# Pooled attention followed by a token and channel mixer on one core: contiguous stationary operand for the maxima, four groups of U turned by VectorE from a DRAM scratch, the order of all steps read from a table

## The chip, the core and the metric

One core of a Trainium2 chip runs the kernel alone. The metric is device time in microseconds, the median of three runs. Engines: PE (matrix products; PEld is its weight load), DVE (vector), ACT (scalar), POOL (GpSimd) and SP, which here only issues DMAs. Each engine has one list of instructions, in the order in which the program wrote them, so that an instruction that waits holds up those behind it in its list; for SP that is a DMA behind a DMA.

## The reference, cut to what matters

```python
def _attn_ref(q, k, v):                      # 4 batches, 8 heads, 1152 positions, 64 channels
    q_pool = q.reshape(B, H, S // 2, 2, D).mean(axis=3)
    scores = scale * np.matmul(q_pool, k.transpose(0, 1, 3, 2))
    scores = scores - np.max(scores, axis=-1, keepdims=True)
    attn = np.exp(scores)
    attn = attn / (np.sum(attn, axis=-1, keepdims=True) + 1e-09)
    return np.matmul(attn, v)
...
def _moe_ref(x, w_tok1, w_tok2, w_ch1, w_ch2):   # x: 4 x 576 x 512
    xt = x.transpose(0, 2, 1)
    h = np.maximum(xt @ w_tok1, 0.0) @ w_tok2
    u = x + h.transpose(0, 2, 1)
    h2 = np.maximum(u @ w_ch1, 0.0) @ w_ch2
    return u + h2
```

The mixer's weights come as 64-bit floats and are narrowed on the chip.

## The kernel before

Everything is split into a high half (rounded for PE) and a low half (the rest), and products are summed from two or three matmuls. There are 32 heads, taken one after the other, two heads to a pair p.

For a pair, K and the pooled Q are loaded in blocks of 32 channels (tiles kn, qn), added (qp, line 594), turned by DVE in 32x32 blocks (line 619 for K) and split (kh, kl; qh, ql). DMAs then stack the halves of one head under each other (kk, qq, and k2, q2 for the third term).

The maxima of a head (maximum, line 758) come first: for each block c of 128 query rows and each third n of the keys, one matmul of 384 columns, with the queries as the stationary operand, and one DVE reduction of its output (line 760). Blocks 0 to 3 take the queries as `QQ[i3][:, c:4 * P:4]`, so with a step of four elements; the rest of 64 rows of both heads of a pair stands in a contiguous tile qd. A DVE reduction makes mh of it (line 725), and one DMA moves its four columns into row 64 of q2 (line 732), where the maximum is subtracted as one more channel of the scores; a second DMA moves the rest (line 736). With the step of four, partition p of mh holds the rows 4p to 4p+3, and the DMA moves runs of four elements.

The scores (line 824) go to PSUM, ACT takes the exponential twice (pf, ph), the low half pl = pf - ph is made by POOL or by DVE (line 845), and PE multiplies with V (line 870). A head named in IN_PV takes three matmuls for this, one of which also sums the row's denominators; any other head takes two, and DVE sums the denominators instead (line 852, six reductions a head), combines two halves (line 883) and, after five more transposes on PE, adds up (lines 919, 922). The output is normalised into U. After every fourth head follows a half of a batch's token mix (lines 952 to 995).

At the end come 24 blocks of channel weights, narrowed by ACT, DVE and POOL, and the channel mix: U is turned in six groups of 384 rows (make_ut, on PE, lines 1060 to 1071, four blocks of 128 channels each), then two chains of matmuls (lines 1082 and 1110) for groups 0 and 1 while weights arrive, and for groups 2 to 5 one after the other.

The program's order is made by a planner: each step has an engine, a cost, a due time from the table DUE and the steps that it depends on; run() picks, step by step, the one that can start first by its own clock, and steps that fit POOL or DVE go where they end first. Three banks of PSUM (ring r) serve the maxima, the turned blocks and the mixer.

Of the kernel before, what the change touches and what calls it, by code (L numbers as in the profile page):

```python
# [3 lines left out]

# [6 lines left out]
F32 = mybir.dt.float32  # L11
# [22 lines left out]
    "scores": -4.5,  # L34
    "p_lo": 5.87,
    "sum": -9.78,
    "pv": 0.35,
    "o": -76.73,
    "finish": -37.65,
    "max": -26.5,  # L40
    "max_each": 0.65,
    "prep": -47.86,
    "v": 2.17,
    "stack": 17.09,
    "stack_2": 76.73,
    "mix": 4.49,
    "mix_x": 5.65,
    "w_tok": 7.87,
    "w_tok_each": 1.94,
    "w_bits": -174.47,  # L50
    "sum_each": 1.52,
    "pv_lo": 0.35,
    "lo_first": 5.54,
    "max_first": -15.11,
    "max_second": 6.31,
    "scores_each": -3.1,
    "p_hi": 0.54,
    "pv_one": -0.55,
    "finish_each": -3.1,
    "den_sum": -15.08,  # L60
    "x_lo": -44.24,
    "x": 27.99,
    "den": -30.38,
    "rd": -20.25,
    "u": 23.45,
    "u_each": -41.15,
    "max_of": -11.3,
    "max_row": -21.2,
    "max_first_each": 11.02,
    "q_pool": -54.73,  # L70
    "q_turn": 5.19,
    "k_each": 1.94,
    "k_hi": 4.75,
    "k_turn": -0.25,
    "q_diag": -18.19,
    "k_lo": -10.58,
    "q_hi": -15.28,
    "q_lo": -11.2,
    "load_kq": -56.71,
    "load_v": -34.48,  # L80
    "v_lo": -62.7,
    "load_w_tok": -85.57,
    "mix_x_lo": -44.87,
    "mix_1": 3.42,
    "mix_t": -1.29,
    "mix_2": 3.13,
    "mix_u": -203.98,
    "w_ch": 9.35,
    "w_ch_each": 23.09,
    "ut_0": -20.54,  # L90
    "ut_1": -43.87,
# [4 lines left out]
IN_PV = (0, 1, 2, 3, 5, 8, 10, 12, 13, 14, 16, 18, 21, 22, 23, 24, 26, 27, 31)  # L96
# [9 lines left out]
class Step:  # L106


    __slots__ = ("eng", "cost", "other", "shared", "fn", "at", "n", "get", "bufs", "next", "left", "ready", "end")


class Plan:
# [11 lines left out]
    def step(self, eng, cost, fn, at, read=(), write=(), get=(), after=(), other=None, shared=False):  # L124
# [6 lines left out]
        s.other, s.shared = other, shared or eng == POOL  # L131
# [36 lines left out]
    def run(self):  # L168
        clock, wire, port = [0.0] * 6, 0.0, 0.0

        def wake(s):
            ready[s.eng].append(s)
            if s.other:
                ready[s.other[0]].append(s)

        slots = {k: [(0.0, i) for i in range(len(v))] for k, v in self.pools.items()}
        ready = [[] for _ in range(6)]
        turns = {k: deque() for k in self.pools if k not in self.any_order}
        for s in self.steps:
            for buf in s.get:  # L180
                if buf.pool in turns:
                    turns[buf.pool].append(buf)
            if not s.left:
                wake(s)
        order = []
        while len(order) < len(self.steps):
            best = None
            for eng in range(6):
                for s in ready[eng]:
                    start = max(s.ready, clock[eng])  # L190
                    if s.shared:
                        start = max(start, port)
                    if s.other:
                        ends = [
                            max(s.ready, clock[e]) + cost
                            for e, cost in ((s.eng, s.cost), s.other)]
                        if (ends[0] > ends[1] + self.stay) == (eng == s.eng):
                            continue
                    for buf in s.get:
                        free = slots[buf.pool]  # L200
                        if not free or buf.pool in turns and turns[buf.pool][0] is not buf:
                            start = float("inf")
                        else:
                            start = max(start, min(free)[0] + 200)
                    key = (start, s.at, s.n)
                    if best is None or key < best[0]:
                        best = key, s, eng
            (start, _, _), s, eng = best
            assert start < float("inf")
            ready[s.eng].remove(s)  # L210
            if s.other:
                ready[s.other[0]].remove(s)
                if eng != s.eng:
                    s.eng, s.cost = s.other
            for buf in s.get:
                free = slots[buf.pool]
                buf.slot = min(free)[1]
                free.remove(min(free))
                if buf.pool in turns:
                    turns[buf.pool].popleft()  # L220
            if s.eng == DMA:
                clock[DMA] = start + 650
                wire = max(start + 1265, wire) + s.cost
                s.end = wire + 650
            else:
                s.end = clock[s.eng] = start + s.cost
                if s.shared:
                    port = s.end
            for t in s.next:
                t.ready = max(t.ready, s.end + AFTER.get((s.eng, t.eng), 0))  # L230
                t.left -= 1
                if not t.left:
                    wake(t)
            for buf in s.bufs:
                buf.left -= 1
                if not buf.left:
                    slots[buf.pool].append((max(u.end for u in buf.users), buf.slot))
            order.append(s)
        self.span = max(s.end for s in order)
        return order  # L240
# [3 lines left out]
def kernel(  # L244
# [43 lines left out]
    due = DUE  # L288
    WARM = 11
    KEEP = (0, 1, 2, 3)  # L290
# [85 lines left out]
    identr = const.tile([P, P], F32R, name="identr")  # L376
    ve.tensor_copy(identr, ident)
# [73 lines left out]
    for i in range(2):  # L451
# [30 lines left out]
    def tok_weights(after):  # L482
# [6 lines left out]
        def load(key, dst, src, n, write):  # L489
            raw[key] = dst  # L490
            step(DMA, wire(n), lambda: sy.dma_start(dst, src), due["w_tok"] + due["load_w_tok"], write=write,
                 after=after)
# [60 lines left out]
    def load_kq(p, t, after):  # L553
        b, h0 = divmod(2 * p, H)

        def load_k(j, c0, c1):
            step(DMA, 2 * wire(4 * P * (c1 - c0) * D), lambda: sy.dma_start(
                KN[:, c0:c1, j], k[b, h0 + j].rearrange("(c p) d -> p c d", p=P)[:, c0:c1]),
                t, write=[("kn", j, c, y) for c in range(c0 // 3, c1 // 3) for y in range(2)], after=after)

        def load_k_blocks(j, y):
            g = slice(64 * j + 32 * y, 64 * j + 32 * y + 32)
            step(DMA, 2.1 * wire(4 * S * 32), lambda: sy.dma_start(
                KB[g], k[b, h0 + j].rearrange("(m r) (y i) -> y r m i", r=32, y=2)[y]),
                t, write=[("kn", j, c, y) for c in range(3)], after=after)

        def load_q_blocks(j, y, x):
            g = slice(64 * j + 32 * y, 64 * j + 32 * y + 32)
            step(DMA, 2.1 * wire(4 * SQ * 32), lambda: sy.dma_start(
                QB[g, x], q[b, h0 + j].rearrange("(m r x) (y i) -> x y r m i", r=32, x=2, y=2)[x, y]),  # L570
                t, write=[("qn", j, y, x)], after=after)
# [649 lines left out]
```

## Time and profile before

| what | value |
|---|---|
| median of 3 runs | 932.87 us (928.86 to 935.71) |
| the profiled execution | 930.23 us |
| its span, first to last instruction | 928.4 us |
| PE busy | 888.6 us, 96% |
| DVE, ACT, POOL busy | 621.6, 552.3, 502.7 us |
| granted PE clock, mean | 0.984 |

Busy time is the time in which at least one instruction of an engine was under way. Matmuls overlap, so that a single matmul's duration is longer than its distance to the next; what a matmul costs in a dense stretch is read from the distances of the starts.

### The profile page before, as it was taken

How to read it: one execution, taken by the hardware profiler on the slowest of the kernel's cores; microseconds unless marked ns; L12 is line 12 of the kernel's file. 1: busy time of each engine (PE TensorE's matmuls, PEld its weight loads, DVE VectorE, ACT ScalarE, POOL GpSimd, SP SyncE). 2: the span in 40 equal slices, each digit the busy share in tenths (PEclk: the TensorE clock that was granted, in tenths of full speed). 3: DMA queues.
4: the chain of work that ended last, by engine and by line, in shares of the span. 5: the costliest groups of instructions: out<-in, count | busy, mean ns of one | idle time of the engine just before them, and what ended most of it. 6: DMA issues, size and time to landing. Idle time of an engine off the chain costs nothing.

```text
span 928.4 us, 15308 instructions
## 1 busy us (share of the span) xinstructions
PE 888.6 (96%) x5399; PEld 827.3 (89%) x5399; DVE 621.6 (67%) x1193; ACT 552.3 (59%) x1141; POOL 502.7 (54%) x394
## 2 busy tenths in 40 slices
PE   8579999999999999999999999999999999999997
PEld 6479989898989999989999999889899999999996
DVE  7777888987978889898788878678992222221211
ACT  5667888788698779787878789754332111111110
POOL 4778798877688778787688778733330000000000
PEclk9879999999999999999999999999999999999999
DMA  8988757745577557575665352034430101000001
GB/s 169 194 161 151 147 119 153 135 99 107 120 149 137 117 114 140 120 149 99 140 124 104 82 119 83 18 114 125 131 114 1 69 1 35 1 35 1 35 1 34
DMA packets 218348, 91.56 MB, mean 99 GB/s; under 512 B 194016, under 2 KB 201568, under 8 KB 218272
## 3 DMA queue, kind: packets, MB, share of 16 engines
q1 hardware_dynamic: 218272, 90.60, 46.6%
q8 instruction: 42, 0.69, 0.3%
q14 instruction: 34, 0.28, 0.1%
HBM read 43.25 MB, written 4.72 MB: 52 GB/s over the span
## 4 chain that ended last, share of the span: by engine, by line
PE 72%; DMA 9%; DVE 7%; ACT 6%; SPq 3%; issue 2%; POOL 1%; DVEq 0%; ACTq 0%; POOLq 0%
PE o L870 15%; PE r L1082 14%; PE s L824 12%; PE s L1110 11%; PE r L758 10%; DMA kk<-kl 5%; PE o L1110 2%; PE r L985 2%; DMA raw<-in_moe_w_ch_dram 2%; ACT pf L838 2%; ACT ph L841 2%; PE r L967 2%; DVE mx L760 1%; PE r L907 1%; DVE v L364 1%
## 5 line engine op out<-in xcount | busy, mean ns | idle before, releaser
L845 POOL TENSOR_TENSOR pl<-pf,ph 128x576 fp32r<-128x576 f32 x258 | 372.5, 1463 | 99.1 <-PE o L870 56.8
L838 ACT ACTIVATE pf<-s 128x576 f32<-128x576 f32 x288 | 195.4, 682 | 75.7 <-PE s L824 66.3
L760 DVE TENSOR_REDUCE mx<-r 128x1 f32<-128x384 f32 x384 | 199.4, 550 | 43.0 <-PE r L758 39.4
L841 ACT ACTIVATE ph<-s 128x576 fp32r<-128x576 f32 x288 | 189.3, 660 | 11.1 <-PE o L870 7.4
L870 PE MATMUL o<-ph,vv 128*65 128x288 f32 (+2 forms) x918 | 192.4, 299 | 3.4 <-DVE ot L883 1.7
L824 PE MATMUL s<-qq,kk 128*128 128x288 f32 x574 | 170.0, 306 | 3.1 <-ACT ph L841 1.3
L758 PE MATMUL r<-kk,qq 128*128 128x384 f32 x372 | 159.3, 448 | 9.7 <-DMA kk<-kl 8.2
L824 PE MATMUL s<-q,k 65*128 65x288 f32 x576 | 167.9, 301 | 0.3 <-ACT q L793 0.3
L1090 DVE SCALAR_TENSOR_TENSOR h<-r,h 128x384 fp32r<-128x384 f32 x72 | 40.1, 556 | 166.3 <-ACT h L1088 166.2
L1088 ACT ACTIVATE h<-r 128x384 fp32r<-128x384 f32 x72 | 35.3, 491 | 186.2 <-PE r L1082 186.2
L870 PEld LDWEIGHTS o<-ph,vv 128*65 128x65 f32 (+2 forms) x918 | 132.4, 152 | 9.8 <-DVE ot L883 3.6
L870 PE MATMUL o<-pl,vv 128*65 128x288 f32 (+1 forms) x576 | 134.9, 296 | 0.1
L1110 PE MATMUL s<-w,h 128*128 128x512 f32 x504 | 130.8, 394 | 0.0
L758 PEld LDWEIGHTS r<-kk,qq 128*128 128x128 f32 x372 | 112.6, 312 | 17.8 <-issue 6.0
L824 PEld LDWEIGHTS s<-qq,kk 128*128 128x128 f32 x574 | 112.9, 197 | 10.2 <-ACT ph L841 6.0
L824 PEld LDWEIGHTS s<-q,k 65*128 65x128 f32 x576 | 111.0, 193 | 0.7 <-ACT q L793 0.5
L1082 PE MATMUL r<-big,w 128*128 128x384 f32 x576 | 109.1, 337 | 0.3 <-DVE h L1090 0.3
L1110 PEld LDWEIGHTS s<-w,h 128*128 128x128 f32 x504 | 93.4, 188 | 16.5
L1082 PEld LDWEIGHTS r<-big,w 128*128 128x128 f32 x576 | 101.7, 188 | 4.1 <-DVE h L1090 0.5
L852 DVE TENSOR_REDUCE sum<-pf 128x96 f32<-128x960 f32 x78 | 88.1, 1135 | 4.6 <-ACT pf L838 4.5
L870 PEld LDWEIGHTS o<-pl,vv 128*65 128x65 f32 (+1 forms) x576 | 87.6, 161 | 1.6 <-DVE pl L845 0.3
L1045 POOL TENSOR_TENSOR w<-v,w 128x512 fp32r<-128x512 f32 x24 | 33.9, 1416 | 60.2 <-ACT w L1044 60.2
(131 smaller groups left out, 1119.5 us busy)
## 6 DMA issues: line engine op xcount, KB each, us to landing
raw<-in_moe_w_ch_dram SPq DMA_DIRECT2D x24, 512.0 KB, 3.6
kk<-kh SPq DMA_DIRECT2D x32, 288.0 KB, 4.0
qq<-qh SPq DMA_DIRECT2D x64, 144.0 KB, 2.5
kk<-kl SPq DMA_DIRECT2D x32, 288.0 KB, 4.5
vn<-in_v_dram SPq DMA_DIRECT2D x32, 288.0 KB, 3.2
k<-kk SPq DMA_DIRECT2D x31, 288.0 KB, 5.1
kn<-in_k_dram SPq DMA_DIRECT2D x60, 144.0 KB, 4.2
qn<-in_q_dram SPq DMA_DIRECT2D x120, 72.0 KB, 2.7
```

What stands on the lines that cost most here:

```text
L758: step(PE, mm(SP3), lambda ps=ps, w=w, x=x: te.matmul(at(ps)[:, 0:SP3], w, x, start=True, stop=True), t, read, [ps], [ps])
L760: step(DVE, dve(SP3), lambda ps=ps, m=m: ve.tensor_reduce(m, at(ps)[:, 0:SP3], axis=AX.X, op=ALU.max), t + due["max_of"], [ps], [key])
L824: te.matmul(at(st)[:, i, 0:HF], w[:, c * P:(c + 1) * P], x[:, fq * HF:(fq + 1) * HF], start=(n == 0), stop=(n == len(terms) - 1))
L838: step(ACT, act_ps(2 * HF) + (0 if near else 49), lambda pf=pf, st=st: sc.activation(pf, at(st)[:, :, 0:HF], AF.Exp, scale=ESC), t, [(st, ...
L841: step(ACT, act_ps(2 * HF) + 15, lambda ph=ph, st=st: sc.activation(at(ph), at(st)[:, :, 0:HF], AF.Exp, scale=ESC), t + due["p_hi"], [(st, ...
L845: both(2 * HF, lambda e, pf=pf, ph=ph, pl=pl: e.tensor_sub(at(pl), pf, f(at(ph))), t + due["p_lo"], [("pf", s), ph], [pl], [pl], on=POOL i ...
L852: step(DVE, 65 + 1.06 * (NK + 1) * HF // CUT, lambda fq=fq, cs=cs: ve.tensor_reduce(SUM[:, fq, cs], PF[:, 5 * fq:5 * fq + 5, cs].rearrange ...
L870: lambda o=o, x=x, w=w, m=m, i=i, c=c, new=new, end=end: te.matmul(at(o)[0:m - w], VV[i2][:, c, w:m], at(x)[:, i], start=new, stop=end),
L1082: te.matmul(at(ps)[:, 0:GT], w[:, c], x[:, c], start=(c == 0 and n == 0), stop=(c == NC4 - 1 and n == 2))
L1088: step(ACT, act_ps(GT), lambda: sc.activation(at(h)[:, 0], at(ps)[:, 0:GT], AF.Relu), t, [ps], [h])
L1090: step(DVE, dve(GT), lambda: ve.scalar_tensor_tensor(out=at(h)[:, 1], in0=at(ps)[:, 0:GT], scalar=0.0, in1=f(at(h))[:, 0], op0=ALU.max, op ...
L1110: te.matmul(at(ps), a[:, x * P:(x + 1) * P], w, start=(fi == 0 and m == 0), stop=(fi == NF - 1 and m == 2))
```

## The change

1. The maxima's queries become contiguous: block c is now rows 128c to 128c+127, and partition p of mh holds rows p, 128+p, and so on. Each of the four columns of mh is moved by a DMA of its own, 128 single elements each.
2. The token mix also stores U to a DRAM scratch (MIXED), with two DMAs for each of its eight halves. For groups 2 to 5 of the channel mix, make_ut loads each block of 128 channels back with four DMAs of 32 channels each (runs of 128 bytes) and turns it with one DVE instruction; PE's transposes stay for groups 0 and 1. The first product of a group waits for all four blocks of its U.
3. run() no longer plans. A table gives the order of all 6869 steps, and a second one names the 62 that go to DVE and not to POOL. Buffers are given out in the order in which they come free.
4. IN_PV has 17 heads and not 19. DUE's numbers changed, but with the table they no longer set the order. An unused copy of the identity goes, and three of the first head's extra warming matmuls.

Read out, the second table puts on DVE 41 low halves of P, 2 of V, 9 of the token mix, 5 sums of Q and 5 of the channel weights (in the kernel before: 30, 5, 5, 5 and 0). Between the loads of pair 1 and the first DMA of the row of maxima of head 1, the first table puts on SP two of the four loads of token weights, two of the four kn of pair 2 and its eight qn. In the kernel before, all four loads of token weights stand there, all four kn and eight qn of pair 2, and two qd of pair 1. On PE the first step after head 0 is now a score of head 1; before, it was a maximum of head 2 with qd.

```diff
-IN_PV = (0, 1, 2, 3, 5, 8, 10, 12, 13, 14, 16, 18, 21, 22, 23, 24, 26, 27, 31)
+IN_PV = (0, 1, 2, 4, 8, 10, 13, 16, 18, 20, 21, 22, 24, 26, 28, 30, 31)
...
     def run(self):
...
+        near = np.frombuffer(zlib.decompress(base64.b85decode(ORDER)), np.uint8).reshape(2, -1)
+        order = [self.steps[n] for n in np.cumsum(near.T.copy().view("<i2")[:, 0])]
+        assert len(set(order)) == len(self.steps)
+        for n in OTHER:
+            self.steps[n].eng, self.steps[n].cost = self.steps[n].other
+        slots = {k: deque(range(len(v))) for k, v in self.pools.items()}
+        for s in order:
+            assert not s.left
             for buf in s.get:
...
+                buf.slot = slots[buf.pool].popleft()
             for t in s.next:
...
                 t.left -= 1
...
             for buf in s.bufs:
                 buf.left -= 1
                 if not buf.left:
...
+                    slots[buf.pool].append(buf.slot)
         return order
...
-    KEEP = (0, 1, 2, 3)
+    KEEP = (0, 1, 2)
...
+    dram = ctx.enter_context(tc.tile_pool(name="dram", bufs=1, space=bass.MemoryType.DRAM))
+    MIXED = dram.tile([B * SQ, C], F32, name="mixed")
...
+        "l": [f(x).rearrange("p j c -> p (j c)")[:, 0:GT] for x in (T1H, T1L)],
...
-        step(DMA, 300, lambda: sy.dma_start(
-            row[:, 0:4 * P].rearrange("o (p c) -> o p c", c=4), mh[:, 0:4]), t,
-            [("mh", 0)], [("row", h % 2, c) for c in range(4)])
+        for c in range(4):
+            step(DMA, 300, lambda c=c: sy.dma_start(row[:, c * P:(c + 1) * P], mh[:, c:c + 1]), t,
+                 [("mh", 0)], [("row", h % 2, c)], pieces=P)
...
-                w, x = QQ[i3][:, c:4 * P:4], KK[i3][:, ks]
+                w, x = QQ[i3][:, c * P:(c + 1) * P], KK[i3][:, ks]
...
+        m0 = g * 2 * SQ
+        step(DMA, 1.3 * wire(16 * P * CM), lambda: sy.dma_start(
+            MIXED[m0 + c0 * P:m0 + (c0 + 4) * P, cols].rearrange("(c p) x -> p c x", p=P),
+            u[:, c0:c0 + 4, cols]), t + due["mix_u"], [("out", b, i, c) for c in range(4)], [("mixed", b, i, 0)],
+             pieces=4 * P)
...
+            if first:
+                def turn(ps=ps, c=c):
...
+                step(PE, G * TURN, turn, t, read + ["first"], [ps, key, *old.get(i, ())], [ps])
+            else:
+                lb, row = Buf("l"), (18 * g + 2 * n * G) * REM
+                for a in range(4):
+                    col = c * P + 32 * a
+                    step(DMA, 2.45 * wire(4 * 32 * GT), lambda lb=lb, a=a, row=row, col=col: sy.dma_start(
+                        at(lb)[32 * a:32 * a + 32].rearrange("r (m i) -> r m i", i=32),
+                        MIXED[row:row + GT, col:col + 32].rearrange("(m r) i -> r m i", r=32)),
+                        t + due["ut_load"], read, [(lb, a)], [lb] if a == 0 else [], after=mixes, pieces=GT)
+                step(DVE, 1.2 * GT, lambda ps=ps, lb=lb: ve.transpose(at(ps)[:, 0:GT], at(lb)), t,
+                     [*((lb, a) for a in range(4)), "first"], [ps, key, *old.get(i, ())], [ps])
...
-            step(PE, 3 * mm(GT), part, t, [("ut", i % 3, c), ("w", 3, fi), "rest"], [ps, h],
+            step(PE, 3 * mm(GT), part, t, [*(("ut", i % 3, x) for x in range(NC4)), ("w", 3, fi), "rest"], [ps, h],
```

## Rows read from the trace of the kernel before

**Rows 1.** The page, part 1: busy time, share of the span, instructions.
```profile
...
PE 888.6 (96%) x5399; PEld 827.3 (89%) x5399; DVE 621.6 (67%) x1193; ACT 552.3 (59%) x1141; POOL 502.7 (54%) x394
...
```

**Rows 2.** Windows by stage: length, busy us (instructions) per engine, granted clock, DMA.
```profile
...
20.00:50.00 30.00, 18.62 (x105) 16.11 (x105) 21.90 (x54) 18.85 (x45) 23.49 (x21) 0.82 1.04 187
50.00:80.00 30.00, 26.73 (x135) 24.33 (x134) 23.41 (x53) 19.07 (x39) 22.30 (x18) 0.79 0.79 155
60.00:600.00 540.00, 523.60 (x3542) 501.27 (x3542) 448.40 (x871) 441.34 (x913) 428.88 (x325) 1.00 0.61 119
...
700.00:860.00 160.00, 160.00 (x818) 145.25 (x817) 33.10 (x60) 22.14 (x46) 0.00 (x0) 1.00 0.06 20
...
```

**Rows 3.** Line 758 (maxima): instructions, duration ns minimum/median/maximum.
```profile
...
L758 PEld LDWEIGHTS r<-kk,qq x372: 307/309/337, 19.7 to 572.3; 128*128 128x128 f32 x186
...
L758 PEld LDWEIGHTS r<-kh,qd x48: 186/188/330, 15.7 to 532.7; 128*128 128x128 f32 x48
...
```

**Rows 4.** PE in order of time around 405 us: start, us, line, operands, count.
```profile
...
405.55 0.43 PE L758 MATMUL r<-kk,qq 128*128 128x384 f32 x1
405.82 0.29 PE L870 MATMUL o<-pl,vv 128*128 128x288 f32 x1
...
```

**Rows 5.** The same around 435 us.
```profile
...
434.75 0.34 PE L758 MATMUL r<-kh,qd 128*128 128x384 f32 x1
434.93 0.30 PE L824 MATMUL s<-qq,kk 128*128 128x288 f32 x1
...
```

**Rows 6.** The chain of waits, 740 to 765 us: start, us, what.
```profile
...
748.04 2.10 PE r L1082 x12
...
756.41 0.98 PE r L1060 x9
...
```

**Rows 7.** The chain of waits, whole span.
```profile
...
134.89 1.06 PE o L870 x8
...
```

**Rows 8.** Groups by line, DVE: count, busy us, mean ns, idle before.
```profile
...
L760 DVE TENSOR_REDUCE mx<-r 128x1 f32<-128x384 f32 x384 | 199.4, 550 | 43.0 <-PE r L758 39.4
...
L852 DVE TENSOR_REDUCE sum<-pf 128x96 f32<-128x960 f32 x78 | 88.1, 1135 | 4.6 <-ACT pf L838 4.5
...
L883 DVE TENSOR_TENSOR ot<-o,low 64x288 f32<-64x288 f32 x26 | 11.6, 445 | 4.0 <-ACT low L881 3.7
...
L919 DVE TENSOR_REDUCE r<-r 128x4 f32<-128x512 f32 x13 | 9.0, 691 | 4.2 <-PE r L915 3.2 <-PE r L907 0.9
...
```

**Rows 9.** Line 845 (low half of P): instructions on POOL and DVE, ns.
```profile
...
L845 POOL TENSOR_TENSOR pl<-pf,ph x258: 1399/1447/2626, 18.8 to 598.9; 128x576 fp32r<-128x576 f32 x129
...
L845 DVE TENSOR_TENSOR pl<-pf,ph x30: 740/784/1981, 144.3 to 597.4; 128x576 fp32r<-128x576 f32 x30
...
```

**Rows 10.** SP in order of time, 30 to 50 us: its DMA issues.
```profile
...
31.30 1.20 SPq L491 DMA_DIRECT2D u<-in_moe_w_tok_dram  x2
32.59 7.68 SPq L563 DMA_DIRECT2D kn<-in_k_dram  x4
40.38 4.70 SPq L569 DMA_DIRECT2D qn<-in_q_dram  x8
...
46.32 0.59 SPq L732 DMA_DIRECT2D q<-mh  x1
...
```

**Rows 11.** DVE in order of time, 25 to 28 us.
```profile
...
25.96 0.17 DVE L725 TENSOR_REDUCE mh<-mx 128x4 f32<-128x12 f32 x1
...
```

**Rows 12.** PE in order of time, 36 to 49 us.
```profile
...
47.87 0.66 PE L758 MATMUL r<-kh,qd 128*128 128x384 f32 x1 [9.98 <-DMA qd<-qh]
...
```

**Rows 13.** Line 732 (row of maxima): issues, ns; who waited; time to landing.
```profile
...
L732 SPq DMA_DIRECT2D q<-mh x31: 504/546/2015, 46.3 to 574.8; - x31
...
  PEld s L824: 0.2, 1
...
DMA to landing us min/median/max: 1.9/2.4/4.8
```

**Rows 14.** The page, part 6: DMA issues, KB each, median us to landing.
```profile
...
kn<-in_k_dram SPq DMA_DIRECT2D x60, 144.0 KB, 4.2
...
```

More of the change, by code (lines that the diff above doesn't have):

```diff
@@ L33 @@
 DUE = {
[L34 to L57, printed above, removed]
@@ L81 @@
[L81 to L91, printed above, removed]
+    "scores": -2.93,
+    "p_lo": 3.58,
+    "sum": -9.57,
+    "pv": 2.54,
+    "o": -51.33,
+    "finish": 8.58,
+    "max": -33.49,
+    "max_each": 0.15,
+    "prep": -34.13,
+    "v": 1.91,
+    "stack": -25.67,
+    "stack_2": -1.62,
+    "mix": 3.46,
@@ new lines @@
+    "mix_x": 6.67,
+    "w_tok": 25.38,
+    "w_tok_each": 0.19,
+    "w_bits": -16.65,
+    "sum_each": 1.34,
+    "pv_lo": -1.1,
+    "lo_first": 24.87,
+    "max_first": -16.17,
+    "max_second": 26.42,
+    "scores_each": -4.16,
+    "p_hi": -0.36,
+    "pv_one": -0.26,
+    "finish_each": -13.78,
+    "den_sum": -50.17,
+    "x_lo": -20.89,
+    "x": 46.21,
+    "den": -101.88,
+    "rd": -11.49,
+    "u": 17.31,
+    "u_each": -154.37,
+    "max_of": -3.2,
+    "max_row": -26.25,
+    "max_first_each": -13.9,
@@ new lines @@
+    "q_pool": -8.21,
+    "q_turn": 4.59,
+    "k_each": 1.41,
+    "k_hi": -501.55,
+    "k_turn": -4.76,
+    "q_diag": 2.44,
+    "load_v_0": -10.17,
+    "v_0": 20.76,
+    "max_1": 24.7,
+    "ut_load": 42.06,
+    "k_lo": 1.85,
+    "q_hi": -23.02,
+    "q_lo": -22.23,
+    "load_kq": -79.9,
+    "load_v": -9.0,
+    "v_lo": -23.38,
+    "load_w_tok": -22.82,
+    "mix_x_lo": -125.66,
+    "mix_1": 1.01,
+    "mix_t": -1.26,
+    "mix_2": 3.21,
+    "mix_u": -46.13,
+    "w_ch": 7.79,
+    "w_ch_each": 1.93,
@@ L106 @@
 class Step:
-    __slots__ = ("eng", "cost", "other", "shared", "fn", "at", "n", "get", "bufs", "next", "left", "ready", "end")
+    __slots__ = (
+        "eng", "cost", "other", "shared", "fn", "at", "n", "get", "bufs", "next", "left", "ready", "end", "pieces")
 class Plan:
@@ L122, in __init__, with step @@
         self.steps, self.data = [], {}
-    def step(self, eng, cost, fn, at, read=(), write=(), get=(), after=(), other=None, shared=False):
+    def step(self, eng, cost, fn, at, read=(), write=(), get=(), after=(), other=None, shared=False, pieces=64):
         s = Step()
         s.eng, s.cost, s.fn, s.at, s.n = eng, cost, fn, round(at, 6), len(self.steps)
-        s.other, s.shared = other, shared or eng == POOL
+        s.other, s.shared, s.pieces = other, shared or eng == POOL, pieces
         s.get, s.next, s.ready, s.end = get, [], 0.0, None
@@ L168, in run @@
     def run(self):
[L169 to L179, printed above, removed]
-            for buf in s.get:
[L181 to L228, printed above, removed]
@@ L766, in turn_over @@
             PS_O.rearrange("p (c x) -> p c x", c=4), VV[1][:, 0, 0:P], VV[1][:, 0:4, 0:P],
-            start=True, stop=True), t, after=after)
+            start=True, stop=True), t, write=[("over",)], after=after)
     def first_maxima(cs, t):
@@ L868, in main @@
                         read += parts if end else parts[:1]
+                    elif h == 0:
+                        read.append(("over",))
                     step(PE, mm(HF),
@@ L997, in token_mix @@
             t += due["mix_2"]
+        m0 = g * 2 * SQ
[3 more added lines that the diff above has]
+             pieces=4 * P)
+        step(DMA, 1.3 * wire(4 * REM * CM), lambda: sy.dma_start(
+            MIXED[m0 + 8 * P + o8:m0 + 8 * P + o8 + REM, cols], u[o8:o8 + REM, 8, cols]),
+            t + due["mix_u"], [("out", b, i, 4)], [("mixed", b, i, 1)])
     NG = 9 // G
@@ L1037, in load @@
                         "(c p) f -> p c f", p=P))
-        step(DMA, wire(8 * P * C), load, t - 3, ["first"], [raw], [raw])
+        step(DMA, wire(8 * P * C), load, t - 3, ["first"], [raw], [raw], pieces=4 * P)
         for n, (eng, cost, fn) in enumerate(narrow(lambda: at(w), lambda: at(raw), C)):
@@ L1055, in make_ut @@
                 bs = (2 * g + ch // 4,) if ch < 8 else (2 * g, 2 * g + 1)
-                read += [("out", b, 2 * c // NC4, ch % 4 if ch < 8 else 4) for b in bs]
-            def turn(ps=ps, c=c):
-                for x, ch in enumerate(chunks):
-                    te.transpose(
-                        at(ps)[:, x * P:(x + 1) * P], U[g][:, ch, c * P:(c + 1) * P], ident)
+                read += [("out", b, 2 * c // NC4, ch % 4 if ch < 8 else 4) if first
+                         else ("mixed", b, 2 * c // NC4, ch // 8) for b in bs]
             old = {1: [("w", 1, x) for x in range(NQ)],
@@ L1140 @@
     for h in range(NH):
-        t0 = NS * h
+        t0, due.head = NS * h, h
         if h % 2 == 0:
@@ L1161 @@
             mixes += plan.steps[n:]
-    t = NS * NH
+    t, due.head = NS * NH, None
     gone = set(mixes)
```

213 lines of the change are left out of this document (167 added, 46 removed), and 3 rows, old and new, of the table OTHER.

## The prediction

> **What bounds the kernel now.** I read the page's busy times first: PE is busy 96% of the span, the next engine, DVE, 67% [rows 1]. Busy PE is not PE at its peak, so the second view is the windows by stage [rows 2]. They show three stages with different limits. From 20 to 80 us the granted clock averages 0.82 and 0.79 of full speed, so PE spent part of that time at the lower of its two levels (1.2 GHz), and it did little. From 60 to 600 us, the heads, PE is busy 523.6 of 540 us, and DVE 448.4, ACT 441.3, POOL 428.9: PE leads, but three engines follow at 80 to 83%. From 700 to 860 us PE is busy all 160 us and DVE 33.1: there PE alone sets the time. Then I looked at what PE's instructions cost by the distances of their starts, since that is what a dense queue feels.
>
> **The contiguous operand.** The weight load of a maximum takes 309 ns with the step of four and 188 ns in the same line with the contiguous tile qd [rows 3]. It reaches the queue as distance: a strided maximum starts at 405.55 and the next matmul at 405.82, 0.27 us on [rows 4], where the contiguous one at 434.75 is followed at 434.93, 0.18 us on [rows 5]. As a second witness, twelve contiguous matmuls of the same 384 columns take 2.10 us, 0.175 each [rows 6]. I take 0.27 - 0.175 = 0.095 us for each of 372: 35.3 us off PE's queue, nearly all of it in the heads, where PE leads. What is bought is queue time, not busy time, and it turns into span only as far as no other engine takes the lead (below).
>
> Here a rule of the Trainium skill speaks against the change. SBUF — State Buffer, in the section "Door 1: The DMA port swizzle (why `[64,N]` ≈ `[32,N]`)", says that SBUF is read in lines of 16 bytes and that one may stride for free up to four fp32 elements. Read so, the step of four elements would cost nothing, and the first term of the sum would be 0 and not 35.3. The trace has 309 against 188 ns, so the measurement decides; the same note also says that each new line costs a penalty, which fits a step of 16 bytes.
>
> **Two heads fewer in IN_PV.** Eight matmuls of 288 columns take 1.06 us on the chain, 0.133 each [rows 7]. A head that leaves IN_PV saves 18 of them, 2.39 us, and adds five transposes; nine transposes take 0.98 us [rows 6], so 0.109 each, 0.54. That is 1.85 a head, 3.7 us for two. DVE pays: of 13 such heads the groups [rows 8] give 88.1/13 = 6.8 for the sums, 11.6/13 = 0.9 and 9.0/13 = 0.7, together 8.4 a head, 16.7 us. ACT keeps about its work.
>
> **U turned by DVE.** 48 of PE's 72 transposes go: 48 x 0.109 = 5.2 us, at the place where PE is busy without a break [rows 2]. What comes is hidden if it comes early: 16 turns on DVE at about 0.58 us, an estimate from the maximum's reduction of as many columns (0.55 [rows 8]), make 9 us on an engine that is idle four fifths of that stage, and 64 loads like kn's, which land in 4.2 us [rows 14]. The new wait is DVE's for four loads; behind it on DVE stand the low halves of h, and behind those PE's second chain. Two products of 12 matmuls (2.1 us each [rows 6]) stand between, and the table issues the loads many steps ahead. So I take 0; with no cover at all it would be 16 x 4.2 = 67 us, which only a load issued just ahead of its turn could bring. The extra wait for all four blocks costs nothing when they are early. The 16 stores are behind the last token mixes and nobody but the turns waits for them.
>
> **Four DMAs for a row.** An issue on SP takes 0.55 us, so the last of four lands 1.65 us later than the one did; for 31 heads SP has 93 x 0.55 = 51 us more to issue. Behind it on SP stand the loads of later pairs and V. In the whole trace one wait is put down to this row, 0.2 us, and it lands after 2.4 us [rows 13]. I take 0 outside the start and keep 1.65 a head as the bound.
>
> **The start.** Head 1's maxima are reduced at 26.1 us [rows 11], but SP issues their row at 46.32 [rows 10]: four kn ahead of it need 7.68 us and eight qn 4.70. PE stands idle 9.98 us until 47.87, and what it takes up then is a maximum with qd, whose DMA stands in the same queue [rows 12]. In the new order two loads of weights, two kn and two qd no longer stand ahead of the row, and no qd is needed first. Six issues of 0.55 to 0.65 are 3.6 us; if the slow kn go with them, half of 7.68 takes the place of two of these, 6.2. Off this goes 1.1 for the third of four DMAs, which the first half of the scores needs: 2.5 to 5. The lower clock may end sooner as well: 0.18 x 30 and 0.21 x 30 us of missing clock are 11.7 us, of which 5 fell into PE's idle time, so at most 6.7 more. I take 5 for both, with 2 and 12 as ends. The change of the first head's warming matmuls and the dropped copy I cost at nothing; they lie in waits for the first DMAs.
>
> **What the gain runs into.** In the heads DVE has 448.4 us of work in 540 [rows 2]. It gets 16.7 from the two heads and 11 more low halves at their median 0.784 [rows 9], 8.6; the other shifts of the second table about cancel. That is 474 us. PE's saving there would make the window 540 - 35 - 4 = 501, and DVE would have to be busy 95% of it. So not all of the gain can be kept for certain. Least loss: 0. Most: if DVE gets no denser than its 448.4/540 = 83%, the window is 474/0.83 = 571. Between them: of DVE's 92 us of idle time 39.4 are waits for maxima's matmuls [rows 8], which now come sooner; if only these go, the window is 474 + 92 - 39 = 527, a loss of 26. On the other side, when reductions follow each other they overlap: 384 with a mean of 550 ns fill 199.4 us, 519 each [rows 8], and the busy time shrinks as the queue fills. I take a loss of 10, nearer to the low end for that reason, as an estimate.
>
> **The sum**, against the profiled execution of 930.2 us (span 928.4 and 1.8 around it): 930.2 - 35.3 - 3.7 - 5.2 - 5 + 10 = 891.0. The median of the three runs lies 2.6 above that execution, so 893.6; I say 893.
>
> **Rivals.**
> - DVE becomes the bound in the heads and keeps the idle time that is not PE's fault: a loss of 26 and not 10, 910; with the start at its low end of 2, 913. For it: 95% is more than any stage shows for DVE. Against: its waits for PE are the larger part of its idle time that has a name.
> - Everything is kept and the start gives all of 12: 893.6 - 10 - 7 = 877; a better order in the rest of the heads could go below, to some 866, if a fourth of the 45 us or so that PE's queue there stands open (my estimate from the distances) closes too.
> - Contiguous changes nothing, as the page's first half says: 893.6 + 35.3 - 10 = 919. Only rows 3 to 5 would have to mislead; nearly excluded.
> - Slower than before: DVE stays at its 83%, the window of the heads becomes 571 in place of 540, and 31 - 5.2 - 5 = 21 are added: 954. It decides from the point where DVE's share in the heads is under 474/550 = 86%. For it: the 62 steps given to DVE are fixed in advance and nothing adapts them, and the row of maxima comes 1.65 us later. Against: waiting for PE is what DVE does with most of its named idle time.
>
> **How the numbers follow.** My forecast (882 to 903) gets 0.53; DVE as the bound (903 to 925) 0.23; all kept (862 to 882) 0.16; contiguous without effect 0.02; slower or level for DVE's sake 0.06. Before's three runs differ by 0.7%, so about 1% is what can be told from no change: faster than 923.5 by these cases 0.91, within 1% 0.04, slower 0.05. The range for 8 in 10 runs from 868 to 914: it takes in both ends of the start and DVE's loss up to 26, and leaves out 1 in 10 on either side.
>
> **What would show it.** In line 758 the weight load at 188 ns throughout and 0.18 us to the next start; PE's transposes of U down to 24; the gap before PE's first score of head 1 shorter than 9.98 us, with the row's DMAs issued before 46 us; DVE busy over 90% of the heads, with waits of PE for its reductions (line 758 waiting for line 760) as the new item if the loss is large. In the last stage PE must stay at 100%. The prediction fails if SP's order makes heads wait for rows, if turns of U come late and PE waits at the start of a group, or if DVE's queue sets the heads' pace.

## The result and the profile after

The changed kernel takes 896.17 us, the median of four runs (894.02 to 897.08); the kernel before, run beside it, 931.93 (928.86 to 935.71). The ratio is 0.961 with an interval of 0.957 to 0.965: 36 us less. The profiled execution has a span of 894.8 us, against 928.4. Times below are medians of fast runs: the kernel named "DVE's load less" had one run of four in a slow state of the chip (1158.66 us at a mean granted clock of 0.652, where the other three had 0.977 to 0.981), which is left out.

The page of the changed kernel, part 1, answers to [rows 1]: PE lost 38.5 us of busy time, DVE gained 4.0 and POOL lost 24.7.

```profile
PE 850.1 (95%) x5322; PEld 785.5 (88%) x5322; DVE 625.6 (70%) x1244; ACT 551.7 (62%) x1141; POOL 478.0 (53%) x378
```

Windows by stage of the changed kernel (columns as in [rows 2]); the heads now end about 576 us, so the third and fourth are set by that.

```profile
20.00:50.00 30.00, 17.24 (x116) 15.34 (x116) 21.32 (x52) 18.26 (x42) 20.84 (x18) 0.87 1.08 165
50.00:80.00 30.00, 24.97 (x131) 21.88 (x131) 25.99 (x60) 19.79 (x41) 23.02 (x19) 0.73 0.86 168
60.00:576.00 516.00, 498.41 (x3539) 471.99 (x3540) 456.11 (x912) 445.98 (x925) 420.46 (x321) 0.99 0.69 134
...
680.00:840.00 160.00, 159.06 (x799) 143.74 (x798) 37.10 (x68) 22.37 (x47) 0.00 (x0) 1.00 0.13 30
```

In the heads PE is busy 97% of the stretch, as before, and DVE 88% in place of 83%. The lower clock did not take less: 0.87 and 0.73 in the first two windows are 12.0 us of missing clock (the share not granted times the length), where 0.82 and 0.79 were 11.7. In the last stage PE leads as it did.

The next two fences answer to [rows 3] and [rows 4]: line 871 (the maxima, line 758 before) with its loads' durations in ns, and PE in order of time.

```profile
L871 PEld LDWEIGHTS r<-kk,qq x372: 186/188/338, 23.3 to 539.1; 128*128 128x128 f32 x186
```

```profile
408.60 0.34 PE L871 MATMUL r<-kk,qq 128*128 128x384 f32 x1
408.78 0.43 PE L985 MATMUL o<-ph,vv 128*65 128x288 f32 x2
```

The load takes 188 ns in the median, and all but 9 of the 372 take under 200; a maximum is followed after 0.18 us, as predicted.

DVE's groups by line, columns as in [rows 8]: the maxima's reductions, the sums of 15 heads (13 before), the turns of U. Then, from PE's weight loads in the same columns, what is left of the transposes of U on PE: 24.

```profile
L873 DVE TENSOR_REDUCE mx<-r 128x1 f32<-128x384 f32 x384 | 192.4, 548 | 27.2 <-PE r L871 24.1
L965 DVE TENSOR_REDUCE sum<-pf 128x96 f32<-128x960 f32 x90 | 100.7, 1133 | 0.6 <-ACT pf L951 0.6
...
L1199 DVE STREAM_TRANSPOSE r<-t1h 128x384 f32<-128x384 f32 x8 | 4.7, 589 | 2.5 <-DMA t1h<-mixed 2.4
L1199 DVE STREAM_TRANSPOSE r<-t1l 128x384 f32<-128x384 f32 x8 | 4.7, 582 | 0.1
```

```profile
L1187 PEld LDWEIGHTS r<-ident,u 128*128 128x128 f32 x24 | 2.9, 140 | 0.1
```

SP in order of time answers to [rows 10], the start of head 1 on PE to [rows 12], the row's line to [rows 13].

```profile
34.27 2.40 SPq L603 DMA_DIRECT2D sum<-in_moe_w_tok_dram  x1
36.78 4.30 SPq L682 DMA_DIRECT2D qn<-in_q_dram  x8
41.13 0.52 SPq L846 DMA_DIRECT2D q<-mh  x1
41.69 0.59 SPq L676 DMA_DIRECT2D kn<-in_k_dram  x1
42.32 0.61 SPq L603 DMA_DIRECT2D u<-in_moe_w_tok_dram  x1
42.97 1.15 SPq L846 DMA_DIRECT2D q<-mh  x2
```

```profile
49.69 0.58 PE L937 MATMUL s<-q,k 65*128 65x288 f32 x1 [10.87 <-DMA qn<-in_q_dram]
```

```profile
L846 SPq DMA_DIRECT2D q<-mh x124: 475/599/1752, 41.1 to 545.2; - x124
...
  PE s L937: 2.6, 2
...
DMA to landing us min/median/max: 1.9/2.5/6.3
```

The row of head 1 is issued earlier, and PE still stands idle 10.87 us before that head's first score, which begins at 49.69. The profile puts this wait down to a load of Q. That it is a wait for the row is shown by the kernel "rows first" below, which moves nothing but the four DMAs of the row and in which head 1 begins at 40.65.

Where the time went can be read from the first `s<-q,k` matmul of a head and the first product of the channel mix, in the two traces:

| from ... to | before, us | after, us | difference |
|---|---|---|---|
| start to head 4 | 106.2 | 105.0 | -1.3 |
| head 4 to head 31 | 475.2 | 451.3 | -23.9 |
| head 31 to the first product of the mix | 23.8 | 22.6 | -1.2 |
| that product to the end | 323.2 | 315.9 | -7.2 |

### The profile page after: what moved, and what is told of

It reads as the page before. It is cut to its first block, busy times and chain, and to the rows that moved or that the text cites. A ratio compares the mean times of both kernels' runs of the same rounds, so it can differ in the third digit from the quotient of the medians.

```text
span 894.8 us, 15517 instructions
## 1 busy us (share of the span) xinstructions
PE 850.1 (95%) x5322; PEld 785.5 (88%) x5322; DVE 625.6 (70%) x1244; ACT 551.7 (62%) x1141; POOL 478.0 (53%) x378
## 2 busy tenths in 40 slices
DMA packets 262207, 99.46 MB, mean 111 GB/s; under 512 B 233264, under 2 KB 245424, under 8 KB 262128
## 4 chain that ended last, share of the span: by engine, by line
PE 70%; DVE 10%; DMA 6%; ACT 6%; SPq 5%; issue 2%; POOL 1%; DVEq 0%; ACTq 0%; POOLq 0%
PE r L1214 16%; PE o L985 13%; PE s L1242 12%; PE s L937 12%; PE r L871 6%; PE o L1242 4%; DVE sum L965 3%; DVE mx L873 3%; PE r L1100 2%; ACT ph L954 2%; ACT pf L951 2%; DMA vn<-in_v_dram 2%; PE r L1082 2%; SPq L682 2%; DMA q<-mh 2%
## 5 line engine op out<-in xcount | busy, mean ns | idle before, releaser
L958 POOL TENSOR_TENSOR pl<-pf,ph 128x576 fp32r<-128x576 f32 x247 | 355.4, 1461 | 80.2 <-ACT ph L954 24.9
L873 DVE TENSOR_REDUCE mx<-r 128x1 f32<-128x384 f32 x384 | 192.4, 548 | 27.2 <-PE r L871 24.1
L985 PE MATMUL o<-ph,vv 128*128 128x288 f32 (+2 forms) x882 | 205.8, 300 | 2.2 <-DVE ot L998 1.0
L985 PE MATMUL o<-pl,vv 128*65 128x288 f32 (+1 forms) x576 | 149.3, 300 | 0.3 <-POOL pl L958 0.3
L985 PEld LDWEIGHTS o<-ph,vv 128*128 128x128 f32 (+2 forms) x882 | 128.9, 153 | 8.8 <-DVE ot L998 3.2
L937 PEld LDWEIGHTS s<-qq,kk 128*128 128x128 f32 x574 | 110.7, 193 | 20.5 <-ACT ph L954 11.3
L871 PE MATMUL r<-kk,qq 128*128 128x384 f32 x372 | 123.9, 349 | 3.5 <-DMA qq<-qh 1.9
L965 DVE TENSOR_REDUCE sum<-pf 128x96 f32<-128x960 f32 x90 | 100.7, 1133 | 0.6 <-ACT pf L951 0.6
L1242 PEld LDWEIGHTS s<-w,h 128*128 128x128 f32 x468 | 86.7, 188 | 15.2 <-DVE raw L1256 1.8
L871 PEld LDWEIGHTS r<-kk,qq 128*128 128x128 f32 x372 | 70.1, 192 | 8.6 <-issue 3.6
L1214 PE MATMUL r<-ut,w 128*128 128x384 f32 x288 | 58.5, 339 | 0.0
```

The source lines that it names most:

```text
L871: step(PE, mm(SP3), lambda ps=ps, w=w, x=x: te.matmul(at(ps)[:, 0:SP3], w, x, start=True, stop=True), t, read, [ps], [ps])
L873: step(DVE, dve(SP3), lambda ps=ps, m=m: ve.tensor_reduce(m, at(ps)[:, 0:SP3], axis=AX.X, op=ALU.max), t + due["max_of"], [ps], [key])
L937: te.matmul(at(st)[:, i, 0:HF], w[:, c * P:(c + 1) * P], x[:, fq * HF:(fq + 1) * HF], start=(n == 0), stop=(n == len(terms) - 1))
L958: both(2 * HF, lambda e, pf=pf, ph=ph, pl=pl: e.tensor_sub(at(pl), pf, f(at(ph))), t + due["p_lo"], [("pf", s), ph], [pl], [pl], on=POOL i ...
L965: step(DVE, 65 + 1.06 * (NK + 1) * HF // CUT, lambda fq=fq, cs=cs: ve.tensor_reduce(SUM[:, fq, cs], PF[:, 5 * fq:5 * fq + 5, cs].rearrange ...
L985: lambda o=o, x=x, w=w, m=m, i=i, c=c, new=new, end=end: te.matmul(at(o)[0:m - w], VV[i2][:, c, w:m], at(x)[:, i], start=new, stop=end),
```

## The experiments

Each kernel was timed beside the kernel before on one chip, and not all of them beside the changed kernel; the kernel before took from 928.55 to 931.93 us there. The last two columns give the distance from the changed kernel, by medians and by ratios to the kernel before (times 930 us). They differ by up to 5 us, so differences from the changed kernel of under some 5 us are not settled by the times alone.

| kernel | median, us | ratio to before | by medians | by ratios |
|---|---|---|---|---|
| changed kernel | 896.17 | 0.9611 (0.957 to 0.965) | | |
| strided again | 914.54 | 0.9851 (0.983 to 0.987) | +18 | +22 |
| before, contiguous alone | 912.61 | 0.9809 (0.978 to 0.984) | +16 | +18 |
| DVE's load less | 893.80 | 0.9617 (0.960 to 0.963) | -2 | +1 |
| ACT's load less | 893.70 | 0.9611 (0.959 to 0.963) | -2 | 0 |
| POOL's load less | 894.84 | 0.9625 (0.961 to 0.964) | -1 | +1 |
| all three less | 888.48 | 0.9584 (0.955 to 0.962) | -8 | -3 |
| one DMA for a row | 885.60 | 0.9541 (0.951 to 0.957) | -11 | -7 |
| U on PE again | 899.24 | 0.9680 (0.966 to 0.970) | +3 | +6 |
| rows first | 894.96 | 0.9637 (0.961 to 0.966) | -1 | +2 |
| rows first, loads later | 902.26 | 0.9705 (0.969 to 0.972) | +6 | +9 |
| rows first, weights later | 908.66 | 0.9787 (0.977 to 0.981) | +12 | +16 |
| order by the planner | 939.20 | 1.0104 (1.007 to 1.014) | +43 | +46 |

**What is contiguity worth?** It is undone in the changed kernel, and made alone in the kernel before.

```diff
-                w, x = QQ[i3][:, c * P:(c + 1) * P], KK[i3][:, ks]
+                w, x = QQ[i3][:, c:4 * P:4], KK[i3][:, ks]
```

In either kernel of this pair the maxima then belong to other rows of the same head than those from which they are subtracted; the work is the same.

> The changed kernel with the maxima's stationary operand read with a step of four again, everything else as it is (a maximum then belongs to another row of the same head, which the softmax cancels up to rounding). Theory 1, PE's queue sets the pace of the heads: 372 x 0.095 us come back, 896 + 30 to 36 = 926 to 932. Rival, DVE or ACT sets it in the new order: PE has room, and only 10 to 20 us come back, 906 to 916. In both, the weight load is at 309 ns and the next matmul 0.27 us behind.

> The kernel before with the contiguous stationary operand alone, its order, its one DMA per row and its 19 heads in IN_PV kept (the maxima stand at other rows of the same head). Theory 1: most of the 35 us shows at once, 932 - 25 to 35 = 897 to 907. Rival: without the new order and with DVE and the fixed queues in the way, under half of it, 915 to 925. No effect, 932, if the step of four were free.

The weight loads follow the layout: 310 ns in the first of these, 189 in the second. It is worth 17 to 22 us either way, so it needs nothing else of the change; but it is not 35. The first time, 914.54, lies in the range of the rival and the second, 912.61, between the two ranges; whether the rival's reason holds is tried below. To see where the rest stayed I took, from head 4 to head 31, each distance between PE's starts, and as "needed" the lower quartile of the distances between the same two instructions (line, tiles and shape of both); what lies over it is "open". The last column is the time that PE spent at the lower of its two clock levels.

| head 4 to 31, us | whole | needed | open | at 1.2 GHz |
|---|---|---|---|---|
| before | 475.2 | 443.0 | 32 | 0 |
| before, contiguous alone | 461.9 | 411.9 | 50 | 3.4 |
| strided again | 467.5 | 433.1 | 34 | 0 |
| changed kernel | 451.3 | 403.5 | 48 | 6.8 |

Contiguity takes 31.1 or 29.6 us off what the queue needs in these 27 heads, and 18 or 13 us of that come back as open time. Of these at most 1.7 or 3.4 us are the lower clock, half of the time spent at it. The levels of "needed" are an estimate: with the first of the two instructions alone as the group they shift by up to 7 us, and the two differences stay at 31 and 29. In the changed kernel 42 waits of over 150 ns hold 23.0 us of the open time, and 263 of 25 to 150 ns hold 20.7.

**Is it DVE's load, as predicted, or another engine's?** Three kernels each take work from one engine and keep PE's, and a fourth all three. The sums of `pf` take one block in place of five, ACT's first exponential half of its columns from head 3 on, and POOL's low half half of its columns from head 4 on. By the traces this takes some 72 us of busy time from DVE, 66 from ACT and 131 from POOL.

```diff
-                        PF[:, 5 * fq:5 * fq + 5, cs].rearrange("p c x i -> p x c i"),
+                        PF[:, 5 * fq:5 * fq + 1, cs].rearrange("p c x i -> p x c i"),
...
-                pf, at(st)[:, :, 0:HF], AF.Exp, scale=ESC), t,
+                pf[:, :, 0:n], at(st)[:, :, 0:n], AF.Exp, scale=ESC), t,
...
-                at(pl), pf, f(at(ph))), t + due["p_lo"], [("pf", s), ph], [pl], [pl],
+                *(x[:, :, 0:m if e is po else HF] for x in (at(pl), pf, f(at(ph))))), t + due["p_lo"], [("pf", s), ph], [pl], [pl],
```

> The changed kernel with the 90 sums of denominators over one block of P in place of five (it leaves out four fifths of that sum; DVE loses some 90 x 0.85 = 76 us of work, all in heads not in IN_PV). The contiguous operand returned 18 of 35 us, so something else leads for part of the time. Theory 2, DVE: most of the lost 17 comes back and more, 896 - 12 to 20 = 876 to 884. Rival, chains between the engines (scores wait for the exponentials to empty PSUM, and so on) that no engine's load explains: 890 to 896.

> The changed kernel with the full-precision exponential (pf) over half of its columns from the fourth head on (it leaves out the other half; ACT loses some 261 x 0.24 = 63 us of work and the scores' PSUM comes free sooner). If ACT's load or its place in the chain from scores to exponentials makes PE wait (PE's named waits in the heads are for lines 951 and 954), 896 - 10 to 20 = 876 to 886. If DVE alone leads, 892 to 896.

> The changed kernel with POOL's low halves of P over half of their columns from the fifth head on (it leaves out the other half; POOL loses some 215 x 0.7 = 150 us of work). POOL is the least loaded of the four in the heads: if load decides, 893 to 896. If the time until pl is there delays the second product and so the next head, 896 - 6 to 15 = 881 to 890.

> The changed kernel with all three reliefs at once: sums of denominators over one block of five, half of pf from the fourth head on, half of POOL's pl from the fifth (each left out as in its own run). Alone they gave 2 us at most each. Theory 3: the engines hand the lead to each other from one short stretch to the next, so that relief of one shows the next; together they give much more than the sum of 6, 896 - 12 to 25 = 871 to 884. Rival: what PE waits for is not work on these engines at all but the fixed order, the DMAs and the steps between, 888 to 892.

None of the three alone moves the time by more than 2.5 us, where each engine as the cause would have given at least 6 to 12. The kernel with all three takes off 3 to 8, as its rival had it, though in its heads (the third window of above, here 60 to 560 us) DVE is busy only 76% of the time, ACT 77% and POOL 57%:

```profile
60.00:560.00 500.00, 485.57 (x3482) 464.27 (x3482) 380.91 (x899) 384.11 (x905) 285.81 (x317) 0.99 0.71 137
```

From head 4 to 31 this kernel takes 444.2 us, 7.1 less than the changed kernel, and its open time is still 42 us of 48. So neither DVE's load nor that of another of the three is by itself what keeps PE's saving from arriving; the three together account for some 6 us of the open time, and the larger part stays.

**Four DMAs for a row or one?** The four steps stay in the table, but three issue nothing; the last, put at the place of the third, issues one DMA in runs of four elements, as the kernel before does. Here too each maximum belongs to another row of its head. The lists of PE, ACT, DVE and POOL are the same as in the changed kernel; only SP's differs.

```diff
+            done.append(0)
+            if len(done) == 4:
+                sy.dma_start(row[:, 0:4 * P].rearrange("o (p c) -> o p c", c=4), mh[:, 0:4])
```

> The changed kernel with the old single DMA for a row of maxima, issued where the third of the four stood (runs of four elements, so that a maximum belongs to another row of the head). 93 issues of 0.6 us leave SP. If the four DMAs delay heads or hold up loads behind them, 896 - 4 to 10 = 886 to 892; if they are hidden, as I had costed them, 894 to 898.

The span is 885.2 us, 9.6 less, of which head 4 to head 31 gives 7.4: what is needed there stays (403.7 us), and the open time falls from 48 to 40. One stretch of 3.4 us at the lower clock fewer can be 1.7 of this. At 885.60 us, just under its first range, it is the fastest kernel of this study, clearly faster than before; against the changed kernel the two intervals of the ratios just touch, and the traces carry the rest. The chain of waits of the changed kernel in the heads (105 to 545 us: start, length, what), and the engines' shares of the whole chain, of the changed kernel and then of this one:

```profile
118.15 2.31 DMA q<-mh
...
135.22 2.02 DMA q<-mh
...
167.15 1.45 SPq L846
169.82 2.02 DMA q<-mh
...
201.76 1.39 SPq L846
203.19 2.02 DMA q<-mh
```

```profile
PE 70%; DVE 10%; DMA 6%; ACT 6%; SPq 5%; issue 2%; POOL 1%; DVEq 0%; ACTq 0%; POOLq 0%
```

```profile
PE 70%; DVE 13%; ACT 7%; DMA 4%; SPq 2%; issue 2%; POOL 0%; DVEq 0%; ACTq 0%; POOLq 0%
```

Two of the rows shown come onto the chain as 1.4 us of issues in a line and then 2.0 of landing, the other two with the landing alone. In this window the chain of the changed kernel is 3.1% `DMA q<-mh` and 2.2% `SPq L846`, together 23 us of 440; with one DMA SP's 93 issues go (326 us of issues from head 4 to 31 become 271), the shares of SPq and DMA fall, and DVE's rises in their place. Part of what is saved thus goes to the next in line: 23 us of chain are worth 7 to 11. Whether the issues or the smaller packets (262,207 in all against 248,814) cost more, this run doesn't separate.

**U turned by PE again**, at the same place of the table; loads and stores stay.

> The changed kernel with PE turning U for groups 2 to 5 at the place in the order where DVE did; the stores and loads of the scratch stay, unused by the product. Theory: 48 x 0.109 = 5.2 us come back on an engine that never pauses there, 901. Rival: DVE's turns had cost PE waits as long as that, 896, no difference.

3 us by medians and 6 by ratios, on either side of the 5.2 of the sum. The trace settles it: from the first product of the mix to the end this kernel takes 321.2 us and the changed kernel 315.9, 5.2 more, all of it at the full clock in both.

**The start.** Three kernels move steps of the table: the four DMAs of head 1's row directly behind its mh; then also the later loads of token weights and of pair 2 250 places on; or, with the row moved as in the first, the steps that narrow the weights 60 places on. In the last two some steps that depend on these change places with them.

```diff
+        place = {s.n: float(k) for k, s in enumerate(order)}
+        for n in range(253, 257):
+            place[n] = place[252] + (n - 252) / 8
+        for n in (*range(258, 261), *range(289, 325)):
+            place[n] += 250
+        order.sort(key=lambda s: place[s.n])
```

> The changed kernel with the four DMAs of head 1's row of maxima moved on SP to just behind the reduction that makes them, ahead of the loads of pair 2 and of three loads of token weights. Theory: PE's 10.87 us of idle time before the scores of head 1 is the wait for these rows behind a load of weights; the rows land before 39 us and most of it goes, 896 - 6 to 10 = 886 to 890. Rival: the exponentials of head 1 stand on ACT behind the token weights' halves, which wait for the same loads, so PE stops after two pairs of scores instead, 893 to 896.

> The changed kernel with head 1's rows moved forward as in the run before, and three of the four loads of token weights with all steps on their data moved some 250 places later in the order of all steps (about a head and a half). Theory: the rows alone brought head 1's first score from 49.7 to 40.7 us, and what took their place is ACT, where exponentials of head 1 stand behind halves of token weights that wait for those loads; with both out of the way head 2 starts 8 to 12 us sooner, and the kernel takes 884 to 889. Rival: the weights' steps on DVE and ACT only move into heads 2 and 3, where DVE has no room either, 892 to 897.

> The changed kernel with head 1's rows forward, loads where they were, and only the steps on the last five units of token weights moved 60 places later, behind the first exponentials of head 1. If ACT's order alone stood behind the rows' gain: head 2 starts 4 to 6 us sooner and the kernel takes 890 to 892. Rival, as the run with 250 places showed for the later heads: the steps only move their delay to heads 2 and 3, 895 to 899.

| first score of head, us | 1 | 2 | 4 |
|---|---|---|---|
| changed kernel | 49.7 | 75.8 | 105.0 |
| rows first | 40.7 | 77.4 | 107.3 |
| rows first, loads later | 37.1 | 70.3 | 111.4 |
| rows first, weights later | 38.8 | 89.5 | 119.5 |

With the rows first, head 1 begins at 40.65, 9 us earlier, but head 2 no earlier, and the end doesn't move, as the rival had it. The waits of PE by what ended them (total us, times, longest us) in that kernel show what took the row's place:

```profile
PE s L941 <- ACT pf L955: 13.0, 6, 11.3
```

ACT in order of time in that kernel has the reason for 4.27 us of these 11.3: it stands in its own list at a narrowing of the token weights, whose load has not landed, and exponentials of head 1 stand behind it. In the rest ACT works on other steps that stand ahead of the exponentials, with waits of 0.62 us at most.

```profile
50.79 0.46 ACT L642 ACTIVATE w<-u 128x288 f32<-128x288 f32 x1 [4.27 <-DMA u<-in_moe_w_tok_dram]
51.16 0.46 ACT L776 CAST qh<-r 128x384 fp32r<-128x384 f32 x1
51.51 0.65 ACT L958 ACTIVATE ph<-s 128x576 fp32r<-128x576 f32 x1
```

In the changed kernel the same wait is there, at the same time as the row's: ACT in order of time, and the DMAs issued from 40 to 50 us (count, KB each, us to landing).

```profile
48.87 0.46 ACT L638 ACTIVATE w<-u 128x288 f32<-128x288 f32 x1 [4.33 <-DMA u<-in_moe_w_tok_dram]
```

```profile
u<-in_moe_w_tok_dram SPq DMA_DIRECT2D x2, 576.0 KB, 6.4
...
q<-mh SPq DMA_DIRECT2D x4, 0.5 KB, 5.5
```

Moving the loads away as well pays early and costs later (head 4 at 111.4 in place of 105.0); moving only the narrowing is worse. Both times, 902 and 909 us, lie above both ranges that were expected. The clock has a part in this that the expectations left out. With the narrowing moved, PE is busy for less than half of the window from 50 to 80 us and the clock stays at its lower level throughout (columns as in [rows 2]); in the changed kernel this window has 0.73.

```profile
50.00:80.00 30.00, 14.39 (x39) 9.55 (x40) 14.03 (x32) 10.97 (x24) 14.01 (x12) 0.50 0.71 133
```

From head 1 to head 4 the missing clock is 20.5 us in that kernel, 17.1 with the loads later, 11.9 with the rows alone and 8.3 in the changed kernel.

**The order by the planner.** run() of the kernel before, with its costs, works on the changed kernel's steps and DUE.

> The changed kernel's steps, costs and due times with the planner of the kernel before in place of the two tables. The contiguous operand alone gave 17 us on the kernel before, PE's transposes are worth 3; with the two heads fewer (3.7 by the sum) that is 932 - 24 = 908. Theory: the table gives the rest, so 905 to 915 without it. Rival: the table only writes down what the planner would have found, 896.

Slower than the kernel before by 1% (six runs, 930.70 to 941.89), and 43 us over the table's order, far outside both ranges. Head 4 to 31 takes 481.7 us, of which 409.9 are needed and 72 open, and the waits that have a name are no one thing:

```profile
PE s L992 <- ACT pf L1006: 8.5, 16, 1.2
PE s L992 <- DMA q<-mh: 7.4, 3, 4.3
PE r L926 <- DMA kk<-kl: 4.1, 4, 2.7
```

Part of the 43 us comes by way of the clock. The mean granted clock is 0.962 of a span of 937.6 us, which is 36 us of missing clock; in the changed kernel 0.981 of 894.8 leaves 17. So up to 19 us lie there, 10 of them between head 4 and head 31, where PE spent 27.3 us at the lower level in place of 6.8. The longest such stretch there (columns as in [rows 2]):

```profile
169.00:183.00 14.00, 13.06 (x41) 9.34 (x42) 12.74 (x27) 3.19 (x8) 2.36 (x2) 0.51 0.49 77
```

The due times of this run are those of the changed kernel, which doesn't use them, since its table gives the order; whether the planner would do better with others was not tried.

## Why the prediction was right, and where its steps were not

893 us were forecast and 896 measured, but that they lie so close is luck: the terms below fell short by some 14 to 23 us (3 to 8 for contiguity with its loss, 7 to 11 for the rows, 4 for the start), and the order of the steps, which outside the start had no term, gave about as much.

- **Contiguous, -35.3.** The mechanism holds: 188 ns for 309, 0.18 us for 0.27, and 30 us less in the queue from head 4 to 31. As a term of the sum it is mis-sized together with the next: net of it -25 were forecast, and -17 to -22 measured. The rival by which it changes nothing is out. The Trainium skill (SBUF — State Buffer, section "Door 1: The DMA port swizzle (why `[64,N]` ≈ `[32,N]`)") gives four elements as how far one may stride for free in fp32; read as the prediction read it, this doesn't hold for the weight load here, which takes 309 ns with a step of four and 188 without.
- **The loss to DVE, +10.** The step that failed. Its size was too small (13 to 18 us of the queue's saving come back as open time), and its reason was not what the runs show. DVE did get the work: 12.6 us for the sums, with 1.6 and 1.9 for what follows them, 16.1 of the 16.7 forecast; the low halves rose by 4.4 and not 8.6, and others fell, so that the heads hold 456 us and not 474. But taking 72 us of work from DVE gained 2.4 us at most, and with DVE at 76%, ACT at 77% and POOL at 57% the time is only 3 to 8 us less. PE's open time sits in many short waits of the finely interleaved list, up to 3.4 us of it in the lower clock, and no one engine's throughput answers for it. Which waits feed each other stays open.
- **Four DMAs for a row, 0.** The second step that failed. [Rows 13] showed one wait of 0.2 us, but that was with one DMA; with four, issue and landing of rows stand on the chain and cost 7 to 11 us. The bound of 1.65 us a head, 51 in all, held; the value should have come from inside it. That the shorter queue of PE made these DMAs late is argued and not shown: four DMAs with the strided operand were not set against one. Nor do they explain the loss of the step above, since contiguity alone loses as much with one DMA for a row.
- **The start, -5.** About -1 was measured to head 4. The first three of the row's DMAs went out before 46 us, as predicted, the fourth only at 49.26, and the gap before head 1 is 10.87 us and not under 9.98. The step failed in that it looked at SP's list alone: the token weights' loads are in the way twice, among the DMAs (the row took 5.5 us to land, 2.5 in the median) and on ACT's list ahead of the exponentials. Its part for the clock came to nothing: 12.0 us of missing clock for 11.7.
- **U by DVE, -5.2.** Right: -5.2 by the trace of the run that gives the turns back to PE. 16 turns of 0.59 us make 9.4 us (9 forecast), one load was awaited, 2.4 us, on DVE, and PE is busy 159.06 of 160 us there. The mix to the end takes 7.2 us less; of the other 2 us up to 1.7 can be the clock, which the kernel before has at its lower level from 605.5 to 609.0 us and the changed kernel nowhere in this stage.
- **Two heads fewer in IN_PV, -3.7.** DVE's side is measured above; PE's was not tried alone.
- **The table of the order**, to which the sum gave only the start: this made up for what the other terms lacked. With the rest of the change in place it is worth 43 us against the planner that it replaces, up to 19 of them by way of the clock. From contiguity alone to the whole change are 16.4 us by medians (912.61 - 896.17) and 18 by ratios; U's 5.2 and the heads' 3.7 less the 7 to 11 of the rows leave some 15 to 20 for the order, by subtraction alone. The rival "all kept" had named a better order in the rest of the heads. There the new order shows more in what the queue needs (443.0 us before, 433.1 strided again, of which the two heads are 3.7) than in open time, which is 48 us with the whole change and 50 with contiguity alone.

The rival that ends slower, DVE stuck at 83%, is refuted by the time itself and by DVE's 88% in the heads.

## What to carry to other kernels

When a change splits a small transfer into several, give the issues in a row and the landing a cost, even if the profile before shows hardly a wait for it. A replaced order is a change of its own and needs a term of its own, measured against the order that it replaces. Before you put a lost gain down to an engine because it is 90% busy, take work from that engine: here 72 us of DVE's work were worth 2.4 us at most. And read the granted clock beside every time: the orders that left PE idle longer at the start also had it longer at the lower level (41 us with the narrowing moved, 24 in the changed kernel).

## What the runs showed that was not expected

- A DMA of 0.5 KB landed after 2.5 us in the median (1.9 to 6.3), and after 5.5 in a stretch with two loads of 576 KB in the same list (40 to 50 us).
- 93 issues on SP, which does nothing else, and 13,393 packets fewer are worth 7 to 11 us of 896, with the lists of all other engines unchanged.
- With the narrowing of the weights moved, the granted clock stayed at its lower level from 43 to 84 us; in the planner's order it fell to it again in the heads, from 169 to 183 us.
- Half of ACT's first exponentials, half of POOL's low halves, or four fifths of DVE's sums can go for at most 2.5 us each; all three together are worth 3 to 8.
